# RWKV-5 attention and a wave MLP on one core: w loaded as one row and spread by a product, with a new order in the opening

## The chip, the cores and the metric

The kernel runs on one core of one Trainium2 chip. The metric is device time in microseconds of one execution, the median over the runs. TensorE is called PE here (PEld is its loading of weights), VectorE DVE, ScalarE ACT, GpSimd POOL, and SyncE SP; SP computes nothing and issues transfers. ACT and POOL issue transfers too, each on its own queue.

## The reference

r, k and v are [4, 8, 768, 48] f32 (batch, heads, tokens, columns of a head), w and u are [8, 48]. The first stage runs a decaying state over the tokens, the second mixes tokens and channels:

```python
for t in range(S):
    cur = np.einsum('bhd,bhe->bhde', u[None] * kt, vt)
    y[:, :, t] = np.einsum('bhd,bhde->bhe', rt, state + cur)
    state = w[None, :, :, None] * state + np.einsum('bhd,bhe->bhde', kt, vt)
...
theta = x @ w_theta                      # x: y as [4, 768, 384]
zr, zi = x * np.cos(theta), x * np.sin(theta)
y = einsum('ts,bsd->btd', w_tok_r, zr) + einsum('ts,bsd->btd', w_tok_i, zi)
u = x + y
return u + np.maximum(u @ w_ch, 0.0)     # f32 [4, 768, 384]
```

## The kernel before

The recurrence is done in blocks. The 768 tokens of a batch element are three pairs of chunks of 128 tokens, and a load brings 256 tokens of all eight heads (384 KB). Within a block the decay is taken off beforehand: k is multiplied by powers of w that fall with the token's place (table `kpow`, or `kpow_c` for pairs laid out in the other way) and r by the inverse ones (`rpow`). The products are `Kw` and `Rw` (L546). PE turns them (`flip`, L484), ACT or DVE copies the turned blocks to `KT` and `RT` (L499, L500), PE forms scores `RT` by `KT` (L592), and DVE masks these into `mAT` (L601). The bonus term with u takes an elementwise product `PD` of `RT` and `KT` (L608, for the first pair on POOL), which PE sums against the columns of u over w, `uw` (L625, the diagonal product). State, outputs, x, theta, sine and cosine, z, the token mixing (L859) and the channel product (L891) follow, batch element after batch element.

The powers are exponentials: `tok_f` holds factors of the token's place, `lw_f` the logarithm of w, and six activations (L388) write exp(factor * log w) into the tables. For that w is loaded onto all 128 partitions, as 128 equal rows (L300, `w_row`, which lies in a buffer of `z`). A second, small load (L395) brings w and u as `wu`, four rows of two heads each; PE turns it (L402, the flip of wu), and from that come `wup`, `uw` (L407, L422) and, on ACT, `lwu` (L410) and `w256`.

Some products do no work: `unread` (L291) multiplies a tile of zeros, six and eight times in the opening (tasks 3 and 4, the warm-ups), and after the tasks named in `IDLE`, as often as its third number says.

The order is written out by hand. Every step is a task with a number, by its place in the source; `ORDER` lists the numbers in the order in which the instructions are issued, each to the queue of its engine; `WAYS` picks one of a task's alternatives by a digit (for L395: 0 is SP, 1 is ACT). `BANKS` gives PSUM banks to PE's tasks in the order in which they ask, and `AFTER` adds waits, such as that of the first cast of weights (task 48, on POOL) for the first loads of r and k (tasks 34 and 35). Each engine works through its queue in order and waits at an instruction until what it needs is there.

Of the kernel before, what the change touches and what calls it, by code (L numbers as in the profile page):

```python
# [14 lines left out]
F32 = mybir.dt.float32  # L15
# [3 lines left out]
Act = mybir.ActivationFunctionType  # L19

PE, DVE, ACT, POOL, SP, NONE = "PE", "DVE", "ACT", "POOL", "SP", "NONE"
# [7 lines left out]


ORDER = [
# [42 lines left out]
]  # L74

WAYS = (
    "000000000000000000000000001100000000000000100101001000010000001001000000000200000010"
    "000000011000000000000000000001000100000000000000100100000100100000000000000000000000"
    "000000000000100000000000000000110000000000002100100000000000000000001000000000000000"
    "000000010000000000000000000100000000000010000000000100000000000000000000011011000000"  # L80
# [17 lines left out]
]  # L98

IDLE = [  # L100
    (3, 0, 1), (4, 1, 3), (71, 2, 2), (116, 6, 3), (76, 1, 3), (49, 4, 2), (51, 1, 1),
    (94, 5, 4), (97, 4, 1), (157, 3, 1),
]

# [59 lines left out]
def rows_of(w, n):  # L164
    return dataclasses.replace(w, ap=[[0, n]] + [list(x) for x in w.ap])
# [13 lines left out]
def kernel(  # L179
# [13 lines left out]
    nc = tc.nc  # L193
    B, H, S, D = r.shape
    HD = H * D
    C = 128
# [7 lines left out]
    sb = ctx.enter_context(tc.tile_pool(name="sb", bufs=1))  # L204
    ps = ctx.enter_context(tc.tile_pool(name="ps", bufs=1, space=bass.MemoryType.PSUM))
    P = Plan()
# [13 lines left out]
    place = sb.tile([C, 2, C], BF16, name="place")  # L220
    mask01 = sb.tile([C, 2, C], BF16, name="mask01")
    zero = sb.tile([C, C], BF16, name="zero")
    col_i = sb.tile([C, C], mybir.dt.int32, name="col_i")
    thr = sb.tile([C, 3], F32, name="thr")
    pi2 = sb.tile([C, 1], F32, name="pi2")
# [46 lines left out]
    def act(n, fn, more=51):  # L272
        return (ACT, n / 1.2 + more, False, fn)
# [21 lines left out]

    def setup():
        if WARM:
            P.add((DVE, 120, False, lambda: nc.vector.memset(zero, 0.0)), wr=["zero"],
                  prio=-3e4, name="zero")
        P.add((ACT, 2950, False, lambda: nc.scalar.dma_start(out=w_row, in_=rows_of(w, C))),  # L300
              wr=["w_row"], prio=-3e4, name="w_row", kind="small")
        P.add((DVE, 60, False, lambda: nc.vector.memset(pi2, math.pi / 2.0)), wr=["pi2"],
              prio=-210, name="pi2")
# [69 lines left out]
        def pads(ts):  # L373
# [4 lines left out]
        P.add(pool(260 * NR, lambda: pads(Rws)), wr=[("Rw", i) for i in range(NR)], prio=-202,  # L378
              name="pads")

        P.add(act(HD, lambda: nc.scalar.activation(
            lw_f, w_row, Act.Ln), 93), rd=["w_row", "set"], wr=["lw_f"], prio=-200,
            name="ln")
        for i, (dst, nm, j, col) in enumerate((
                (kpow, "kpow", 0, 2), (kpow, "kpow", 1, 3), (rpow, "rpow", 0, 0),
                (rpow, "rpow", 1, 1), (kpow_c, "kpow_c", 0, 5), (kpow_c, "kpow_c", 1, 6))):
            to = dst[:, j] if nm[-1] == "c" else dst[:, :, j, :]
            P.add((ACT, 510, False, lambda to=to, col=col: nc.scalar.activation(  # L388
                to, lw_f, Act.Exp, scale=tok_f[:, col:col + 1])),
                rd=["lw_f", "tok_f"], wr=[(nm, j), ("exp", i)],  # L390
                prio=-199 + 0.1 * i, name="pow")

        for i, src in enumerate((w, u)):
            def wu_load(eng, i=i, src=src):
                return eng.dma_start(out=wu[i * HP:(i + 1) * HP, :, :D],  # L395
                                     in_=src.rearrange("(a b) d -> a b d", b=2))
            P.add([(SP, 450, False, lambda f=wu_load: f(nc.sync)),
                   (ACT, 2700, False, lambda f=wu_load: f(nc.scalar))], rd=["wu0"],
                  wr=[("wu", i)], prio=-90 + 0.0035, desc=(0, 1, 20), name="wu", kind="small")

        def wu_flip():
# [557 lines left out]
```

## Time and profile before

| What | us |
|---|---|
| median of two runs | 141.53 |
| lowest and highest | 141.36, 141.69 |
| span of the profiled execution, from its first to its last instruction | 139.4 |
| busy in that span: PE, DVE, ACT | 126.8, 112.0, 78.4 |
| busy in that span: POOL | 60.4 |
| start of the first scores on PE (L592) | 13.69 |
| last instruction of the first setup on DVE before it waits for PE | 4.54 |

The profile gives the span of the execution it shows and no other time for it; the runs' median lies 2.1 us above that span. PE is busy for 91% of the span, and the granted clock in its rows is 1.00 throughout. How to read the lines below: an instruction row gives its start, its length, engine, line, operation, output<-input and count, and in brackets how long the engine had stood idle and for whom. `x3` counts instructions. In a row of issues the last number is the time from issue to landing.

### The profile page before, as it was taken

The page shows a single profiled execution, that of the slowest core. Times are in us where ns is not written, and L with a number is a line of the kernel's source. Part 1 is how long each engine was busy: PE and PEld are TensorE (multiplying, and loading weights), DVE is VectorE, ACT ScalarE, POOL GpSimd, SP SyncE. Part 2 cuts the span into 40 slices and gives each one's busy share as a digit, 9 for nine tenths or more (in the row PEclk, how much of TensorE's full clock was granted, in tenths as well). Part 3 has the DMA queues.
Part 4 walks back from the last instruction along what each step waited for, and adds up shares of the span by engine and source line. Part 5 has one row for each costly group of instructions (what it writes and reads, how often), then busy time and mean ns, then how long its engine had stood idle before and what let it go on. Part 6 is the DMA issues. An engine that isn't in the chain of part 4 may idle for free.

```text
span 139.4 us, 4508 instructions
## 1 busy us (share of the span) xinstructions
PE 126.8 (91%) x1896; PEld 83.5 (60%) x1896; DVE 112.0 (80%) x207; ACT 78.4 (56%) x147; POOL 60.4 (43%) x63
## 2 busy tenths in 40 slices
PE   1775999899798999999999999999999999999980
PEld 0134657677464777676766667776566675666630
DVE  5329998797989999899966979999989997256470
ACT  2466369987760657898895779556501351810110
POOL 5025776735423069999300059997302722000000
PEclk9999999999999999999999999999999999999999
DMA  3999999999999995039799998969993718605344
GB/s 35 247 253 251 267 250 263 219 236 228 234 268 244 271 135 78 5 121 261 195 168 229 207 203 147 158 142 119 314 208 104 152 34 211 172 0 169 61 164 175
DMA packets 64941, 25.08 MB, mean 180 GB/s; under 512 B 59416, under 2 KB 64920, under 8 KB 64920
## 3 DMA queue, kind: packets, MB, share of 16 engines
q1 hardware_dynamic: 62320, 21.63, 73.2%
q0 software_dynamic: 2432, 2.95, 12.7%
q10 hardware_dynamic: 168, 0.20, 1.4%
q8 instruction: 15, 0.25, 0.8%
q14 instruction: 6, 0.05, 0.1%
HBM read 20.25 MB, written 4.72 MB: 179 GB/s over the span
## 4 chain that ended last, share of the span: by engine, by line
PE 77%; DVE 8%; DMA 4%; ACT 3%; POOL 2%; issue 2%; ACTq 0%; POOLq 0%; DVEq 0%
PE bank L859 31%; PE bank L484 10%; PE bank L891 8%; PE bank L822 8%; PE bank L592 4%; DMA wu<-in_w_dram 4%; PE bank L658 3%; PE bank L747 3%; DVE Rw L546 2%; PE bank L625 2%; PE bank L799 2%; PE bank L763 2%; PE bank L734 2%; POOL PD L608 2%; DVE z L837 1%
## 5 line engine op out<-in xcount | busy, mean ns | idle before, releaser
L859 PE MATMUL bank<-z,WrT 128*128 128x384 bf16 x144 | 46.8, 326 | 0.7 <-DVE z L837 0.7
L859 PE MATMUL bank<-z,WiT 128*128 128x384 bf16 x144 | 46.8, 326 | 0.0
L634 POOL TENSOR_TENSOR yd<-dg,vb 128x768 bf16<-128x768 f32 x11 | 16.2, 1471 | 7.3 <-ACT vb L568 3.2
L859 PEld LDWEIGHTS <-WiT 128*128 128x128 bf16 x144 | 14.1, 98 | 8.4 <-issue 0.8
L859 PEld LDWEIGHTS <-WrT 128*128 128x128 bf16 x144 | 14.0, 98 | 8.3 <-ACT WrT L499 0.3
L601 DVE TENSOR_TENSOR mAT<-bank,mask 128x512 bf16<-128x512 f32 x28 | 18.1, 680 | 0.1
L608 POOL TENSOR_TENSOR PD<-RT,KT 128x1024 bf16<-128x1024 bf16 x5 | 10.6, 2124 | 15.4 <-ACT dg L630 14.3
L877 DVE TENSOR_TENSOR uu_all<-bank,x 128x384 bf16<-128x384 f32 x24 | 13.1, 552 | 4.8 <-PE bank L859 4.4
L837 DVE TENSOR_TENSOR z<-x,trig 128x1536 bf16<-128x1536 bf16 x12 | 13.0, 1081 | 4.9 <-ACT trig L829 2.6
L499 ACT ACTIVATE KT<-bank 128x1024 bf16<-128x1024 bf16 x11 | 11.2, 1022 | 8.1 <-PE bank L484 7.8
L829 ACT ACTIVATE trig<-bank,pi 128x384 f16<-128x384 f32 x24 | 13.6, 583 | 2.7 <-PE bank L822 2.5
L833 ACT ACTIVATE trig<-bank 128x384 f16<-128x384 f32 x24 | 11.3, 490 | 6.3 <-PE bank L822 6.3
L822 PE MATMUL bank<-Wth,xT 128*128 128x384 bf16 x72 | 14.3, 326 | 0.0
L891 PE MATMUL bank<-Wch,uu_all 128*128 128x384 bf16 x72 | 13.8, 326 | 0.1
L601 DVE TENSOR_TENSOR mAT<-bank,mask_c 128x512 bf16<-128x512 f32 x20 | 13.0, 681 | 1.1 <-PE bank L592 0.9
L291 PE MATMUL bank<-zero 128*128 128x512 bf16 x35 | 10.7, 430 | 3.0 <-DVE thr L338 3.0
L499 ACT ACTIVATE RT<-bank 128x1024 bf16<-128x1024 bf16 x10 | 10.2, 1021 | 5.2 <-PE bank L484 5.2
L900 DVE SCALAR_TENSOR_TENSOR fin_all<-bank,uu_all 128x384 f32<-128x384 f32 x22 | 11.4, 550 | 0.9 <-PE bank L891 0.8
L546 POOL TENSOR_TENSOR Kw<-ld,kpow 128x768 bf16<-128x768 f32 x3 | 7.8, 2588 | 6.2 <-DMA ld<-in_k_dram 4.7
L592 PE MATMUL bank<-RT,KT 64*64 64x128 bf16 (+1 forms) x304 | 8.8, 220 | 1.3 <-ACT RT L499 1.1
L891 PEld LDWEIGHTS <-uu_all 128*128 128x128 bf16 x72 | 6.6, 97 | 4.2 <-ACT uu_all L499 0.5
L822 PEld LDWEIGHTS <-xT 128*128 128x128 bf16 x72 | 6.5, 98 | 4.0 <-DMA xT<-x 0.4
(111 smaller groups left out, 216.1 us busy)
## 6 DMA issues: line engine op xcount, KB each, us to landing
ld<-in_r_dram SPq DMA_DIRECT2D x12, 384.0 KB, 6.5
out_dram<-fin_all SPq DMA_DIRECT2D x11, 384.0 KB, 3.0
ld<-in_k_dram SPq DMA_DIRECT2D x7, 384.0 KB, 7.5
ld<-in_v_dram SPq DMA_DIRECT2D x7, 384.0 KB, 5.9
ld<-in_k_dram SPq DMA_DIRECT2D x10, 192.0 KB, 4.8
ld<-in_v_dram SPq DMA_DIRECT2D x10, 192.0 KB, 4.7
uu_all<-in_moe_w_tok_r_dram POOLq DMA_DIRECT2D x1, 384.0 KB, 7.2
z<-in_moe_w_tok_i_dram POOLq DMA_DIRECT2D x1, 384.0 KB, 6.5
```

The lines of the kernel that those rows point to most:

```text
L484: ins = [nc.tensor.matmul(bank16(tok)[:, i * C:(i + 1) * C], s, ident, is_transpose=True, start=(i == 0), stop=(i == n - 1)) for i, s in e ...
L499: ways = [act(n * C, lambda: nc.scalar.activation(dst, src(), Act.Copy)), dve(n * C, lambda: nc.vector.tensor_copy(dst, src()), 1.0 if pai ...
L592: ins.append(nc.tensor.matmul(to[:, hp * C:(hp + 1) * C], a, m, start=(hp == 0), stop=(hp == HP - 1), skip_group_check=True))
L601: mask01[:, j] if pairs else mask_c): nc.vector.tensor_mul(
L608: return eng.tensor_mul(flat[2], flat[0], flat[1])
L634: return eng.tensor_mul(yd.rearrange("p a b d -> p (a b) d"), wide(dg, D), vb.rearrange("p a b d -> p (a b) d"))
L822: ins = [nc.tensor.matmul(bank(th)[:, :HD], xT[:, t, dk, :], Wth[:, dk, :], start=(dk == 0), stop=(dk == ND - 1)) for dk in range(ND)]
L829: P.add(act(HD, lambda th=th, t=t, trig=trig: nc.scalar.activation(trig[:, t, 0], bank(th)[:, :HD], Act.Sin, bias=pi2), 144), use=[th], rd ...
L837: P.add(dve(4 * HD, lambda trig=trig, pr=pr: nc.vector.tensor_mul(z[:, 2 * pr:2 * pr + 2], bc(x[:, 2 * pr:2 * pr + 2], 2, 2), trig), 2.0, ...
L859: ins.append(nc.tensor.matmul(bank(tm)[:, :HD], (WrT, WiT)[ri][:, so, to * C:(to + 1) * C], z[:, so, ri], start=(part == 0 and i == 0), st ...
L877: P.add(dve(HD, lambda tm=tm, t=t, to=to, un=un: nc.vector.tensor_add(un[:, t], bank(tm)[:, :HD], x[:, to])), use=[tm], rd=[("x", xi, pr, ...
L891: ins = [nc.tensor.matmul(bank(tf)[:, :HD], uT[:, t, dk, :], Wch[:, dk, :], start=(dk == 0), stop=(dk == ND - 1)) for dk in range(ND)]
```

## The change

The log of w is now computed from one row on one partition, and a product with a row of ones spreads it over all 128 partitions into a PSUM bank (bank 7). The six table activations read that bank. The two small loads of `wu` go from ACT's queue to POOL's.

```diff
 ORDER = [
-    1, 18, 35, 14, 27, 7, 34, 6, 17, 8, 110, 5, 9, 0, 10, 3, 26, 13, 15, 16, 109, 19, 28, 20,
+    1, 18, 34, 14, 7, 35, 6, 17, 8, 36, 5, 9, 0, 10, 3, 27, 26, 13, 15, 11, 16, 109, 19, 4, 20,
...
 WAYS = (
-    "000000000000000000000000001100000000000000100101001000010000001001000000000200000010"
+    "000000000000000000000000002200000000000000100101001000010000001001000000000200000010"
...
 IDLE = [
-    (3, 0, 1), (4, 1, 3), (71, 2, 2), (116, 6, 3), (76, 1, 3), (49, 4, 2), (51, 1, 1),
+    (3, 0, 1), (71, 2, 2), (116, 6, 3), (76, 1, 3), (49, 4, 2), (51, 1, 1),
...
+    ones = sb.tile([1, C], F32, name="ones")
...
-            P.add((DVE, 120, False, lambda: nc.vector.memset(zero, 0.0)), wr=["zero"],
+            P.add((DVE, 120, False, lambda: (nc.vector.memset(ones, 1.0),
+                                             nc.vector.memset(zero, 0.0))), wr=["zero"],
                   prio=-3e4, name="zero")
-        P.add((ACT, 2950, False, lambda: nc.scalar.dma_start(out=w_row, in_=rows_of(w, C))),
+        P.add((ACT, 2950, False, lambda: nc.scalar.dma_start(out=w_row[:1], in_=rows_of(w, 1))),
...
-        P.add(act(HD, lambda: nc.scalar.activation(
-            lw_f, w_row, Act.Ln), 93), rd=["w_row", "set"], wr=["lw_f"], prio=-200,
-            name="ln")
+        lw = bank_t[7][:, :HD]
+
+        def spread():
+            a = nc.scalar.activation(lw_f[:1], w_row[:1], Act.Ln)
+            nc.tensor.matmul(lw, ones, lw_f[:1].rearrange("p h d -> p (h d)"), start=True,
+                             stop=True)
+            return a, a
+        P.add(act(HD, spread, 93), rd=["w_row", "set", "zero"], wr=["lw_f"], prio=-200,
+              name="ln")
...
-                to, lw_f, Act.Exp, scale=tok_f[:, col:col + 1])),
+                to, lw.rearrange("p (h d) -> p h d", h=H), Act.Exp,
+                scale=tok_f[:, col:col + 1])),
...
             P.add([(SP, 450, False, lambda f=wu_load: f(nc.sync)),
-                   (ACT, 2700, False, lambda f=wu_load: f(nc.scalar))], rd=["wu0"],
+                   (ACT, 2700, False, lambda f=wu_load: f(nc.scalar)),
+                   (POOL, 900, False, lambda f=wu_load: f(nc.gpsimd))], rd=["wu0"],
```

In the rows below the lines of the changed kernel are its own; the numbers behind names tell buffers apart, and those of rings stand one higher in the changed kernel.

ACT's queue from the start to the copies of the first turned blocks, before and then changed (`z` is the buffer of `w_row` and `lw_f`, `bank_68` is bank 7):

```order
L300 DMA z_156<-in_w_dram 128x384
L395 DMA wu<-in_u_dram 4x2x48
L310 ACT_TABLE_LOAD
L395 DMA wu<-in_w_dram 4x2x48
L381 ACTIVATE z_156<-z_156 128x384
L388 ACTIVATE kpow<-z_156,tok_f 128x8x48
L388 ACTIVATE kpow_c<-z_156,tok_f 128x384
L410 ACTIVATE lwu<-bank_61 128x4
L388 ACTIVATE rpow<-z_156,tok_f 128x8x48
```

```order
L302 DMA z_157<-in_w_dram 1x384
L312 ACT_TABLE_LOAD
L386 ACTIVATE z_157<-z_157 1x384
L396 ACTIVATE kpow<-bank_68,tok_f 128x8x48 x2
L396 ACTIVATE rpow<-bank_68,tok_f 128x8x48 x2
L420 ACTIVATE lwu<-bank_62 128x4
L509 ACTIVATE KT_121<-bank_62 128x1024
L509 ACTIVATE RT_117<-bank_63 128x1024
L396 ACTIVATE kpow_c<-bank_68,tok_f 128x384 x2
```

The loads of `wu` are gone from ACT, both parts of `kpow` and of `rpow` come first, `lwu` comes behind them, and `kpow_c` behind the copy to `RT`. `KT`'s bank, 62, is now the one that `lwu` reads.

DVE's queue from `uw`'s memset to the first masked scores, before and then changed:

```order
L362 MEMSET uw 128x4
L366 MEMSET Sd_142 128x192
L366 MEMSET Sd_143 128x192
L366 MEMSET Sd_144 128x192
L366 MEMSET Sd_145 128x192
L407 COPY wup<-bank_61 128x4
L422 TENSOR_TENSOR uw<-bank_61,wup 64x4 x2
L546 TENSOR_TENSOR Kw_106<-ld_88,kpow 128x8x2x48
L546 TENSOR_TENSOR Rw_104<-ld_89,rpow 128x8x2x48
L346 TENSOR_SCALAR mask_72<-col_i,thr 128x128 x2
L546 TENSOR_TENSOR Kw_107<-ld_91,kpow 128x8x2x48
```

```order
L364 MEMSET uw 128x4
L348 TENSOR_SCALAR mask_72<-col_i,thr 128x128 x2
L368 MEMSET Sd_143 128x192
L368 MEMSET Sd_144 128x192
L368 MEMSET Sd_145 128x192
L368 MEMSET Sd_146 128x192
L417 COPY wup<-bank_62 128x4
L432 TENSOR_TENSOR uw<-bank_62,wup 64x4 x2
L556 TENSOR_TENSOR Kw_107<-ld_89,kpow 128x8x2x48
L556 TENSOR_TENSOR Rw_105<-ld_90,rpow 128x8x2x48
L556 TENSOR_TENSOR Kw_108<-ld_92,kpow 128x8x2x48
```

The masks move ahead of the memsets, and Kw of pair 1 follows Rw of pair 0 directly.

POOL's queue, from the last pad to the first products, before and then changed:

```order
L374 MEMSET Kw_108 128x16x16
L374 MEMSET Kw_109 128x16x16
L453 DMA uu_all<-in_moe_w_tok_r_dram 128x2x768
L546 TENSOR_TENSOR Rw_105<-ld_92,rpow 128x8x2x48
L608 TENSOR_TENSOR PD_123<-RT_116,KT_120 128x1024
```

```order
L376 MEMSET Kw_109 128x16x16
L376 MEMSET Kw_110 128x16x16
L404 DMA wu<-in_u_dram 4x2x48
L404 DMA wu<-in_w_dram 4x2x48
L463 DMA uu_all<-in_moe_w_tok_r_dram 128x2x768
L556 TENSOR_TENSOR Rw_106<-ld_93,rpow 128x8x2x48
L618 TENSOR_TENSOR PD_124<-RT_117,KT_121 128x1024
```

The two loads of `wu` stand ahead of the first cast of weights. On POOL, Rw of pair 1 waits by semaphore for Rw of pair 0 on DVE, and PD for Kw of pair 1, in both kernels.

On PE, before: seven products with zeros, the flip of `wu`, eleven more with zeros, then K's flip. Changed: seven with zeros, the product that spreads log w, eight with zeros, the flip of `wu`, then K's flip, which takes the bank of the flip of `wu` and so waits for `lwu`. SP's queue begins with the loads r, k, r, k, v, k, v before and with k, r, v, k, r, v, k in the changed kernel; from the eighth load on both are the same, as is everything on the other engines behind the places shown.

2 rows, old and new, of the table ORDER are left out of this document.

## The prediction

> **What bounds the kernel now.** I read the page's head first, then busy time by stretches of ten microseconds, then the chain of work that ended last, then the five engines' timelines of the opening, and the DMA view last.
>
> ```profile
> span 139.4 us, 4508 instructions
> ```
>
> ```profile
> 0.00:10.00 10.00, 5.29 (x18) 1.95 (x19) 3.44 (x27) 4.18 (x8) 2.82 (x13) 1.00 0.83 176
> 10.00:20.00 10.00, 8.25 (x159) 5.37 (x158) 9.97 (x14) 5.45 (x12) 6.24 (x6) 1.00 1.16 257
> ...
> 30.00:40.00 10.00, 9.14 (x120) 6.23 (x120) 9.19 (x11) 7.29 (x15) 4.70 (x4) 1.00 1.13 234
> ...
> 50.00:60.00 10.00, 10.00 (x202) 7.07 (x199) 9.56 (x17) 7.41 (x14) 9.75 (x9) 1.00 0.38 45
> ```
>
> After the stretch's length come the busy times of PE, PEld, DVE, ACT and POOL, then clock, DMA share and GB/s. From 50 us on PE has no gap, so whatever the opening gains or loses by then goes through to the end. The change touches only the opening, up to the first scores. The chain there:
>
> ```profile
> 2.50 5.25 DMA wu<-in_w_dram
> ...
> 7.88 0.21 PE bank L402
> ...
> 9.42 0.51 ACT kpow L388
> ...
> 10.83 0.95 DVE Rw L546
> 11.78 1.98 DVE mask L346 x2
> 13.76 0.88 DVE Kw L546
> ...
> 14.77 2.13 POOL PD L608
> ...
> 16.95 0.35 PE bank L625 x8
> ```
>
> It begins with the load of w's columns, lands at 7.75, and by the flip (L402) and the tables reaches Kw of pair 0. Then Rw, the masks, Kw of pair 1, PD on POOL and the diagonal product (L625) follow. I compare that product's start, 16.95, before and after, since PE stands almost without a gap behind it.
>
> **The change part by part.** Edits with one answer first. The `ones` memset delays `zero` and so the warm-up products.
>
> ```profile
> 3.70 0.84 DVE L366 MEMSET Sd<- 128x192 uint32 x4
> ```
>
> A memset of 192 columns takes 0.21, so 128 columns cost at most that; I take 0.1. Two of w's tables (kpow_c) move behind RT's copy on ACT, where ACT idles before KT of pair 1; they cost nothing, and about 1.0 if that gap closed. v of pair 0 goes ahead of k and r of pair 1, so r becomes the fifth load.
>
> ```profile
> 15.80 1.02 ACT L499 ACTIVATE KT<-bank 128x1024 bf16<-128x1024 bf16 x1 [2.15 <-PE bank L484]
> ```
>
> ```profile
> 7.08 1.37 SPq L433 DMA_DIRECT2D ld<-in_v_dram  x1
> ```
>
> ```profile
> ld<-in_v_dram SPq DMA_DIRECT2D x1, 384.0 KB, 5.8
> ```
>
> The fifth load now is that v: 7.08 + 5.8 = 12.9. Less the 0.75 by which the stream comes forward (below) r lands at 12.15, just before POOL can take it at 12.3: free, with little to spare.
>
> *w as one row.* The 128-row load is what moved first:
>
> ```profile
> q10 hardware_dynamic: 93, 0.12, 50.2%
> q1 hardware_dynamic: 638, 0.24, 46.9%
> ```
>
> This is the DMA from 3 to 5 us: ACT's queue (q10) still holds half of it, SP's loads (q1) share the rest. One row lands earlier, but w's landing isn't on the path any more, because the product that spreads it stands on PE behind seven warm-up products:
>
> ```profile
> 2.97 3.17 PE L291 MATMUL bank<-zero 128*128 128x512 bf16 x7 [2.97 <-DVE thr L338]
> ...
> 8.01 2.55 PE L291 MATMUL bank<-zero 128*128 128x512 bf16 x11
> ```
>
> They end at 6.14 + 0.1 = 6.25, less a short drain: the spread starts at 6.15. No f32 product of 384 columns is in this trace. The lower end is a bf16 one, 0.33 (row L859); the upper end is three early warm-up products, 3 x 3.17/7 = 1.36. I take 0.75, nearer the lower, since the warm-ups quicken from 0.45 to 0.23 each by 8.01: 6.9.
>
> ```profile
> L859 PE MATMUL bank<-z,WrT 128*128 128x384 bf16 x144 | 46.8, 326 | 0.7 <-DVE z L837 0.7
> ```
>
> The Trainium skill, "FP8 and Floating Point Precision", TensorE Precision Notes, says a true FP32 product makes four passes through the array. By it an estimate would be 4 x 0.33 = 1.3, against 0.75, and everything below stood 0.55 later; no row here shows it.
>
> *Eight warm-ups, then the flip.* Eight at 2.55/11 = 0.23 take 1.85 (3.6 if the clock stayed low): PE is free for the flip at 8.75. The four exps that Kw and Rw need start at 6.9 and take 0.5 each on ACT (the chain's 0.51), ending at 8.95, early enough. From the flip's start to uw's end the rows say:
>
> ```profile
> 8.31 0.34 DVE L422 TENSOR_TENSOR uw<-bank,wup 64x4 bf16<-64x4 f32 x2
> 9.96 0.96 DVE L546 TENSOR_TENSOR Kw<-ld,kpow 128x768 bf16<-128x768 f32 x1 [1.30 <-ACT kpow L388]
> ```
>
> 8.65 - 7.88 = 0.77, so uw ends at 9.52 and Kw, which stands behind it on DVE, starts at 9.55 instead of 9.96. lwu waits for uw on ACT, and K's flip now waits for lwu, since both use one PSUM bank: 9.75, well before Kw's end. So the tables' gain of about one us is cut to 0.4 by the flip, which comes behind eight warm-ups.
>
> *wu by GpSimd.* POOL issues both when its last pads are written.
>
> ```profile
> 1.59 1.05 POOL L374 MEMSET Kw<- 128x256 bf16 x4
> ...
> 9.26 0.89 POOL L453 DMA_DIRECT2D uu_all<-in_moe_w_tok_r_dram  x1 [6.61 <-DMA ld<-in_k_dram]
> ```
>
> ```profile
> Wth<-in_moe_w_theta_dram POOLq DMA_DIRECT2D x1, 288.0 KB, 7.6
> Wch<-in_moe_w_ch_dram POOLq DMA_DIRECT2D x1, 288.0 KB, 4.2
> ```
>
> Second issue at 2.64 + 0.85 = 3.5. Landing is 4.2 after issue at the least for a cast, 7.6 in a loaded queue. A transfer of 1.5 KB should be nearer 4.2: 7.7, one us before PE is free. That cover is thin; the ends are 7.7 and 11.1, and below 7.7 nothing is gained. The first cast behind them on POOL waits for loads anyway.
>
> *Masks early.* Two mask operations of 0.28 go where DVE stood idle from the last memset's end, 4.54, to the flip, 7.88: free. In their old place they cost 1.98, and the reason matters:
>
> ```profile
> L346 DVE TENSOR_SCALAR mask<-col_i,thr x2: 281/1074/1868, 11.7 to 11.9; 128x128 bf16<-128x128 int32 x2
> ```
>
> ```profile
> 11.88 1.80 POOL L546 TENSOR_TENSOR Rw<-ld,rpow 128x768 bf16<-128x768 f32 x1 [1.72 <-DVE Rw L546]
> ```
>
> The second mask took 1.87 because POOL was writing Rw of pair 1 from 11.88 to 13.68. That block changes sides. Kw of pair 1 now follows Rw of pair 0 on DVE at once, while POOL's Rw still waits for that Rw's semaphore. What happens then stands later in the trace:
>
> ```profile
> 50.97 1.80 DVE L546 TENSOR_TENSOR Rw<-ld,rpow 128x768 bf16<-128x768 f32 x2
> 52.70 0.68 DVE L608 TENSOR_TENSOR PD<-RT,KT 128x1024 bf16<-128x1024 bf16 x1
> ```
>
> ```profile
> 51.06 4.00 POOL L546 TENSOR_TENSOR Kw<-ld,kpow 128x768 bf16<-128x768 f32 x1
> ```
>
> DVE began first, and POOL's operation took 4.00 instead of 1.80: it stood until DVE's three were through. So Rw of pair 0 ends at 9.55 + 1.82 (9.96 to 11.78 now) = 11.37, Kw of pair 1 at 12.27, POOL's Rw runs 12.3 to 14.1, and PE's flip of it starts at 14.15. Now it starts at 14.04:
>
> ```profile
> 14.04 0.62 PE L484 MATMUL bank<-ident,Rw 128*128 128x128 bf16 x8
> ...
> 16.04 0.82 PE L291 MATMUL bank<-zero 128*128 128x512 bf16 x3
> ```
>
> Between that flip and the diagonal product PE has 2.82 us of its own work (14.04 to 16.86), fillers included, so the product starts at 16.97 against 16.95. The opening gains nothing: 0.4 won on the tables, lost on the port.
>
> *Loads earlier.* 191 of 192 KB of w are no longer moved. At 257 GB/s, the stretch from 10 to 20, that brings the stream of loads forward by 0.75; q10's hold on the engines before 5 us may add as much. It can pay where a load is waited for:
>
> ```profile
> 20.93 3.07 SPq L433 DMA_DIRECT2D ld<-in_k_dram  x1
> ```
>
> ```profile
> ld<-in_k_dram SPq DMA_DIRECT2D x1, 384.0 KB, 13.4
> ```
>
> ```profile
> 34.47 1.80 POOL L546 TENSOR_TENSOR Kw<-ld,kpow 128x768 bf16<-128x768 f32 x1 [1.42 <-PE bank L484]
> ```
>
> ```profile
> 35.01 2.08 DVE L546 TENSOR_TENSOR Rw<-ld,rpow 128x768 bf16<-128x768 f32 x1
> ```
>
> ```profile
> 37.14 0.62 PE L484 MATMUL bank<-ident,Rw 128*128 128x128 bf16 x8 [0.60 <-DVE Rw L546]
> ```
>
> The k load issued at 20.93 lands at 34.33, POOL starts on it at 34.47, and DVE's Rw behind it takes 2.08 instead of 0.95; PE waits 0.60. With the load 0.75 earlier DVE's Rw ends up to 0.75 sooner. I take 0.5, between nothing (POOL meets another DVE operation) and PE's 0.60. What is late next there is z on DVE.
>
> **Sum.** Opening 0.0, loads -0.5: span 138.9. The median of the two runs, 141.53, lies 2.1 above the span of the profile; the page gives no other time for that execution, so I carry the 2.1: **141.0**.
>
> **Rivals.**
> *The columns land late (slower).* Place: POOL's two issues. The Trainium skill, "SBUF — State Buffer", section "SBUF: two separate sides", says that a DMA issued by GpSimd cannot write its descriptors while VectorE holds the shared port pair in a two-port mode, and tells of 620 ns growing to 3100. For it here: POOL and DVE do block each other in the rows above, and DVE runs without a pause until 4.54, in the change 0.6 longer for masks and ones. Against: no issue in the rows above is longer than 0.89. As a mechanism here: both issues start at 5.15, the second at 6.0, landing 4.2 later at 10.2; the flip at 10.3, uw's end 11.05, Kw 11.1 instead of 9.96. POOL's Rw then ends at 15.65, the product comes at 18.5, 1.55 late; less 0.5: **142.5**. It decides from a landing later than about 9.2, which puts Kw back at 10.1. The same follows from a slow spread and a clock that stays low, 8.75 becoming 10.5.
> *POOL takes the port first.* If Rw on POOL starts at 11.4, before Kw of pair 1, it ends at 13.2; the flip comes 2.26 behind Rw of pair 0 as now (11.78 to 14.04), at 13.63, the product at 16.45: 0.5 gained. With the loads' full 0.75 and part of PE's later waits, **140.1**. The start order of the rows speaks against it.
> *The change doesn't do what it says.* The earlier loads meet DVE elsewhere, and the opening is even: **141.5**.
>
> **How the numbers follow.** Forecast 0.5 (own range 140.4 to 141.5), late columns 0.15, POOL first 0.15, nothing 0.2. The range 139.7 to 142.4 holds all of the forecast and of nothing, most of POOL first and not quite half of the late columns. A difference under 2%, 2.8 us, is about what a measurement of this kernel cannot tell from no change. Below 138.7 lies only a tail of POOL first, 0.03; above 144.4 a tail of late columns (11.1 and the low clock together), 0.02; within 2%, 0.95.
>
> **What would show it.** In the changed profile: the spread on PE at 6.1 to 6.2 and its length; the flip at 8.7 to 9.0, started by PE and not by a DMA; Kw on DVE at 9.5; two masks of 0.28; POOL's Rw of pair 1 ending behind Kw of pair 1, about 14.1, with 2.7 on its row instead of 1.80; the diagonal product near 17.0; POOL's Kw at 33.7 instead of 34.47. I'm wrong if the flip waits for wu (first rival), if POOL's Rw ends before 13.5 (second), or if PE's gaps after 20 us change by more than the 0.5 given to the loads.

## The result, and the profile after

The changed kernel takes 148.04 us (147.15 and 148.93), the kernel before 141.53: a ratio of 1.044 (1.036 to 1.053). Six more runs later gave a median of 148.41 (147.02 to 153.41). The forecast was 141.0. A ratio compares undisturbed runs of the two kernels; medians and ranges below are of all runs, and of its 62 later runs the kernel before, too, had four at 147.8 to 148.5, of which no trace was kept.

Busy time by stretches, changed kernel (length; busy time of PE, PEld, DVE, ACT, POOL; clock, DMA share, GB/s):

```profile
0.00:10.00 10.00, 6.90 (x15) 2.24 (x16) 3.43 (x26) 3.80 (x6) 4.15 (x15) 1.00 0.97 208
10.00:20.00 10.00, 6.88 (x93) 4.17 (x91) 6.71 (x11) 4.17 (x7) 5.99 (x4) 1.00 1.23 258
...
30.00:40.00 10.00, 5.89 (x121) 4.45 (x122) 8.81 (x10) 5.52 (x12) 6.66 (x7) 1.00 1.08 233
40.00:50.00 10.00, 8.70 (x70) 6.25 (x69) 7.15 (x9) 5.45 (x10) 0.43 (x1) 0.83 0.92 201
50.00:60.00 10.00, 10.00 (x173) 7.28 (x172) 9.39 (x18) 4.18 (x6) 2.27 (x3) 1.00 0.15 24
```

There are two losses. From 10 to 20 PE does 6.88 where it did 8.25, and from 30 to 40 5.89 where it did 9.14, with a clock of 0.83 behind that. From 50 on PE is full, as before. The chain shows both places:

```profile
7.84 3.49 PE bank L292 x8
12.09 0.96 DVE Kw L556
13.05 0.88 DVE Rw L556
14.01 2.45 POOL Rw L556
...
29.69 1.19 issue
...
35.67 5.59 DVE z L847
```

The warm-ups stand on the path where a load stood, and z takes 5.59 us. The opening on PE:

```profile
3.10 3.17 PE L292 MATMUL bank<-zero 128*128 128x512 bf16 x7 [3.10 <-DVE thr L340]
6.20 1.65 PE L387 MATMUL bank<-z,ones 1*128 1x384 f32 x2
7.78 3.56 PE L292 MATMUL bank<-zero 128*128 128x512 bf16 x8
11.26 0.22 PE L412 MATMUL bank<-ident_f,wu 8*128 8x8 f32 x1
...
19.16 0.34 PE L635 MATMUL bank<-uw,PD 128*128 128x2 bf16 x8
```

The eight warm-ups take 0.44 each, as at half clock, and not 0.23; the flip of wu starts at 11.26 and the diagonal product at 19.16, 2.2 later than before. The clock column says 1.00 all the same; here the length of equal products tells the clock, the column does not.

The second place: z on DVE before, z on DVE after, then POOL and PE after.

```profile
31.80 0.95 DVE L837 TENSOR_TENSOR z<-x,trig 128x1536 bf16<-128x1536 bf16 x1
```

```profile
35.59 5.66 DVE L847 TENSOR_TENSOR z<-x,trig 128x1536 bf16<-128x1536 bf16 x1
```

```profile
33.95 1.48 POOL L644 TENSOR_TENSOR yd<-dg,vb 128x768 bf16<-128x768 f32 x1 [3.25 <-ACT dg L640]
35.36 0.77 POOL L463 DMA_DIRECT2D z<-in_moe_w_tok_r_dram  x1
36.12 0.72 POOL L463 DMA_DIRECT2D x<-in_moe_w_tok_i_dram  x1
36.86 3.56 POOL L556 TENSOR_TENSOR Kw<-ld,kpow 128x768 bf16<-128x768 f32 x2
```

```profile
41.30 0.32 PE L869 MATMUL bank<-z,WrT 128*128 128x384 bf16 x1 [4.51 <-DVE z L847]
```

POOL's two Kw run without a gap; before they stood 1.42 and 4.72 us apart from what preceded them, waiting for loads (the row of the first names a bank of PE, but its load landed at 34.33, just before its start at 34.47). z ends at 41.25, which is 0.83 after the second Kw ends (36.86 + 3.56 = 40.42). PE stands 4.51 for it.

Why the loads are there is seen at SP's start, the third and fourth load before and after:

```profile
1.88 3.91 SPq L433 DMA_DIRECT2D ld<-in_r_dram  x1
5.83 1.21 SPq L433 DMA_DIRECT2D ld<-in_k_dram  x1
```

```profile
1.87 1.01 SPq L443 DMA_DIRECT2D ld<-in_v_dram  x1
2.92 1.29 SPq L443 DMA_DIRECT2D ld<-in_k_dram  x1
```

With w's 128 rows in the transfers the third load's issue took 3.91 and held everything behind it; with one row it takes 1.01, and the fourth to the thirteenth load go out 2.4 to 3.0 earlier. The k load of POOL's first Kw, further on:

```profile
18.00 1.44 SPq L443 DMA_DIRECT2D ld<-in_k_dram  x1
```

```profile
ld<-in_k_dram SPq DMA_DIRECT2D x1, 384.0 KB, 7.2
```

It lands at 25.2; before it landed at 34.33.

From span to span, 139.4 to 147.2: the diagonal product starts 2.2 later, from there to the first product of the token mixing it takes 22.1 instead of 16.0, and from there to the end 105.9 instead of 106.5.

### The profile page after: what moved, and what is told of

It is laid out like the page before. It is cut to its first block, busy times and chain, and to the rows that moved or that the text cites. A ratio compares the mean times of both kernels' runs of the same rounds, so it can differ in the third digit from the quotient of the medians.

```text
span 147.2 us, 4507 instructions
## 1 busy us (share of the span) xinstructions
PE 130.4 (89%) x1895; PEld 85.7 (58%) x1895; DVE 113.0 (77%) x208; ACT 78.5 (53%) x147; POOL 62.0 (42%) x65
## 3 DMA queue, kind: packets, MB, share of 16 engines
HBM read 20.06 MB, written 4.72 MB: 168 GB/s over the span
## 4 chain that ended last, share of the span: by engine, by line
PE 83%; DVE 9%; POOL 2%; issue 2%; ACT 1%; DVEq 0%; POOLq 0%
PE bank L869 33%; PE bank L494 11%; PE bank L901 8%; PE bank L292 7%; PE bank L832 7%; PE bank L602 5%; DVE z L847 4%; PE bank L668 3%; PE bank L757 2%; PE bank L635 2%; POOL Rw L556 2%; PE bank L809 2%; PE bank L773 1%; DVE mAT L611 1%; PE bank L744 1%
## 5 line engine op out<-in xcount | busy, mean ns | idle before, releaser
L869 PE MATMUL bank<-z,WrT 128*128 128x384 bf16 x144 | 47.3, 329 | 4.5 <-DVE z L847 4.5
L869 PE MATMUL bank<-z,WiT 128*128 128x384 bf16 x144 | 47.3, 329 | 0.0
L847 DVE TENSOR_TENSOR z<-x,trig 128x1536 bf16<-128x1536 bf16 x12 | 16.5, 1377 | 4.9 <-ACT trig L843 2.4
L292 PE MATMUL bank<-zero 128*128 128x512 bf16 x32 | 11.7, 496 | 3.1 <-DVE thr L340 3.1
L556 POOL TENSOR_TENSOR Rw<-ld,rpow 128x768 bf16<-128x768 f32 x4 | 7.9, 1974 | 6.8 <-DVE Rw L556 6.8
L602 PEld LDWEIGHTS <-KT 64*64 64x64 bf16 (+1 forms) x304 | 6.1, 103 | 5.4 <-issue 4.8
L691 POOL CAST Sd<-F 64x192 bf16<-64x192 f32 x3 | 1.0, 342 | 19.1 <-ACT F L710 17.1
```

What stands on the lines that cost most here:

```text
L292: ins = [nc.tensor.matmul(bank_t[k][:, :wide * C].rearrange("p (a c) -> p a c", a=wide), zero, bc(zero, 1, wide), start=True, stop=True, s ...
L602: ins.append(nc.tensor.matmul(to[:, hp * C:(hp + 1) * C], a, m, start=(hp == 0), stop=(hp == HP - 1), skip_group_check=True))
L847: P.add(dve(4 * HD, lambda trig=trig, pr=pr: nc.vector.tensor_mul(z[:, 2 * pr:2 * pr + 2], bc(x[:, 2 * pr:2 * pr + 2], 2, 2), trig), 2.0, ...
L869: ins.append(nc.tensor.matmul(bank(tm)[:, :HD], (WrT, WiT)[ri][:, so, to * C:(to + 1) * C], z[:, so, ri], start=(part == 0 and i == 0), st ...
```

## The experiments

The theories: **A**, the opening is late because the flip of wu, and on DVE Kw behind it, stand behind warm-ups that run at half clock. **B**, z loses the port to POOL's two Kw, which are ready too early (port is here, as in the prediction, the name for what makes operations of DVE and POOL wait for each other in its rows); **B2**, they are ready early because the 128-row load is gone. **C**, rival of B: z is late only because the opening is. **D**, the clock comes up by windows of 3.41 us that run free of the kernel. In `ORDER` 3 and 4 are the warm-ups, 19 ln and the spread, 28, 29, 33 and 30 the flip of wu, wup, uw and lwu, 24 and 25 kpow_c, 69 to 74 Kw and Rw of pair 0 and their flips; 108 and 151 are the first two z, 236 and 368 POOL's two Kw.

**The flip of wu first** (`BANKS` exchanges the second and third bank with it).

```diff
-    1, 18, 34, 14, 7, 35, 6, 17, 8, 36, 5, 9, 0, 10, 3, 27, 26, 13, 15, 11, 16, 109, 19, 4, 20,
-    21, 110, 22, 23, 28, 29, 33, 30, 48, 69, 111, 70, 71, 152, 113, 72, 73, 74, 24, 112, 25,
+    1, 18, 34, 14, 7, 35, 6, 17, 8, 36, 5, 9, 0, 10, 3, 27, 26, 13, 15, 11, 16, 109, 19, 28, 4, 20,
+    21, 110, 22, 23, 29, 33, 30, 48, 69, 111, 70, 71, 152, 113, 72, 73, 74, 24, 112, 25,
```

> The changed kernel with the flip of wu issued ahead of the eight warm-ups instead of behind them. Theory A (PE's in-order queue: the flip stands behind eight warm-ups of 0.44 us): the flip starts at 7.8 to 8.0, where the spread product ends, uw ends at 8.6, and Kw of pair 0 is bound by its tables (kpow ends 8.9), so it starts near 9.0 instead of 12.09. The eight warm-ups then run from about 8.1 to 11.6, so PE's flip of Kw starts at 11.6 instead of 13.20: 1.6 us off the opening. Rival (wu's columns come late, not the order): the flip still starts near 11. For the second loss, theory B (POOL's two Kw, ready behind its casts, take the shared port ahead of z on DVE, whatever the opening does): z of the first batch element's first pair is blocked again for more than 3 us and the time is 145 to 147. Rival C (the stall of z comes from the late opening alone): z takes 0.95 and the time is 141 to 142.

Median 145.26 (140.28 to 146.40, 4 runs). In the profile the flip starts at 8.09, Kw at 8.96, and the diagonal product at 17.24, 1.9 earlier: A holds. z took 0.96, which is not what B expected here, yet this run took 144.62, which is not what C expected: this profile fits neither. PE stood 1.11 us within its scores at 27.3, and the clock was at half from 28.6 to 32.0.

**z before POOL's first Kw.**

```diff
-    (34, 48), (35, 48), (70, 113), (112, 82), (155, 85), (168, 134), (406, 559), (448, 565),
+    (34, 48), (35, 48), (108, 236), (70, 113), (112, 82), (155, 85), (168, 134), (406, 559), (448, 565),
```

> The changed kernel with one wait more: the first Kw on POOL after its casts (the one at 36.86) waits for z of the first pair on DVE (the one at 35.59 that took 5.66 us). Theory B (the shared port: z stood behind two Kw of POOL that were ready at once): z takes 0.95 or less from the end of its trig table, PE's idle stretch of 4.51 us shrinks below 0.7, the granted clock stays at 1.00 between 40 and 46, and the time is 142.5 to 144.0, 4 to 5.5 us under the changed kernel. Rival (z waited for something else, the port is only where it shows): z stays at 4 us or more, the time at 147 to 149. The opening is untouched: Kw of pair 0 at 12.1 in either.

Median 144.23 (141.32 to 144.91, 4 runs), 4 under the changed kernel. z took 0.95 and POOL's Kw still follow the casts at once:

```profile
35.39 0.95 DVE L847 TENSOR_TENSOR z<-x,trig 128x1536 bf16<-128x1536 bf16 x1
```

The diagonal product stays at 19.24. B holds: the wait that was added costs POOL nothing and takes the second loss away. POOL's two casts still stand ahead of Kw, the first 0.23 before z, so it was Kw, and not the issuing of the casts, that kept z.

**w over 128 rows again, no spread.**

```diff
-        P.add((ACT, 2950, False, lambda: nc.scalar.dma_start(out=w_row[:1], in_=rows_of(w, 1))),
+        P.add((ACT, 2950, False, lambda: nc.scalar.dma_start(out=w_row, in_=rows_of(w, C))),
...
-        lw = bank_t[7][:, :HD]
...
+            lw_f, w_row, Act.Ln), 93), rd=["w_row", "set"], wr=["lw_f"], prio=-200,
...
-                to, lw.rearrange("p (h d) -> p h d", h=H), Act.Exp,
+                to, lw_f, Act.Exp,
```

> The changed kernel without the spread product: w is loaded onto 128 partitions again and ln runs over 128 rows; the order, the loads, the warm-ups and POOL's queue stay as changed. ln then starts when the load lands, near 5.7, and the eight warm-ups follow the seven at about 6.2 without a break. Theory A1 (the spread product keeps the clock low, being one row of 128 in f32): the eight warm-ups come up to speed within 1 to 2 us, the flip of wu starts between 8.0 and 9.0 and Kw of pair 0 by 9.8. Theory A2 (the clock comes up at a time of its own, whatever PE does): the eight still run at 0.44 us each, the flip starts at 9.7 and Kw at 10.5. The second loss by theory B stays in both (146 to 147); by rival C (it comes from the late opening) it goes, 141 to 143.

Median 142.36 (141.30 to 148.65, 10 runs), 1.003 of before (1.000 to 1.006). So all of the loss hangs on w as one row. Fifteen warm-ups took 4.78 us; the flip waits for wu until 9.04. POOL waits for its loads again (the first row names PE; its load landed at 35.0):

```profile
35.16 1.80 POOL L550 TENSOR_TENSOR Kw<-ld,kpow 128x768 bf16<-128x768 f32 x1 [1.91 <-PE bank L488]
41.70 1.96 POOL L550 TENSOR_TENSOR Kw<-ld,kpow 128x768 bf16<-128x768 f32 x1 [4.73 <-DMA ld<-in_k_dram]
```

I had expected theory B's loss to stay here, and by that expectation this run speaks for C: the order of the loads, which this kernel keeps, isn't what makes Kw ready. B2 and C are told apart further down.

**The order of the loads alone**, in the kernel before.

```diff
-    1, 18, 35, 14, 27, 7, 34, 6, 17, 8, 110, 5, 9, 0, 10, 3, 26, 13, 15, 16, 109, 19, 28, 20,
-    4, 24, 36, 29, 33, 30, 23, 21, 22, 48, 69, 152, 25, 70, 71, 111, 11, 113, 72, 73, 74, 112,
+    1, 18, 34, 14, 27, 7, 35, 6, 17, 8, 36, 5, 9, 0, 10, 3, 26, 13, 15, 16, 109, 19, 28, 20, 4,
+    24, 110, 29, 33, 30, 23, 21, 22, 48, 69, 111, 25, 70, 71, 152, 11, 113, 72, 73, 74, 112,
```

> The kernel before with one part of the change: SP issues its first nine loads in the changed order (k, r, v of pair after pair). Nothing else is touched. Theory B in its strict form (earlier k loads alone make POOL's two Kw ready at once, and z is blocked): z of the first pair on DVE takes more than 3 us and the time is 144 to 146. Rival (the order of the loads changes little, since the Kw of before wait for loads that are issued much later): 141 to 142, with z at 0.95.

Median 141.97 (141.25 to 149.48, 10 runs), 1.002 of before (0.999 to 1.005). The order is harmless. But in this profile, with no spread, the eleven later warm-ups took 4.46 us instead of 2.55: a late clock is not the spread's alone.

**The changed kernel again.**

> The changed kernel once more, unchanged, in more runs, since its time so far rests on two. Theory D (the time depends on when the clock comes up, and that on a window of 3.41 us that runs free of the kernel: the trace's clock record has the clock of the changed kernel up at 11.17, down at 41.89, nine windows later, and up again at 45.30): the runs spread over groups, near 141 where the clock is up before the eight warm-ups, near 144 where it is not, and 147 to 149 where PE also stands still long enough to lose the clock; the median falls to 143 to 145. Rival (148 is the kernel's own time, given by its order): all runs between 147 and 149.

Median 148.41 (147.02 to 153.41, 6 runs), 1.041 of before (1.036 to 1.046). The rival is nearer, and D in this form is wrong: no run was near 141 or 144, but three of the six took more than the rival's 149. z took 5.53 in this profile too.

**The spread first**, 19 moved ahead of 3.

```diff
-    1, 18, 34, 14, 7, 35, 6, 17, 8, 36, 5, 9, 0, 10, 3, 27, 26, 13, 15, 11, 16, 109, 19, 4, 20,
+    1, 18, 34, 14, 7, 35, 6, 17, 8, 36, 5, 9, 0, 10, 19, 3, 27, 26, 13, 15, 11, 16, 109, 4, 20,
```

> The changed kernel with the spread product moved ahead of the seven warm-ups, so that all fifteen warm-ups run without a break behind it, from about 4.8. Theory D with the rider that the spread product does not count as work for the clock: a stretch of 6.5 us of warm-ups fills some window wherever that begins, so the clock is up before the last warm-up in every run, at 10.7 at the latest; the flip of wu starts at 9.6 to 11.0 (11.26 as changed), the tables are done at 7.0, Kw of pair 0 at 10.0 to 11.8; time 141 to 143.5. Rival (the clock comes up at 11 whatever PE does before): the flip at 11.3, Kw at 12.1, the time as the changed kernel's.

Median 147.36 (146.62 to 148.15, 4 runs), 1.042 of before (1.035 to 1.049). The opening did what was expected, the time did not:

```profile
4.72 5.00 PE L292 MATMUL bank<-zero 128*128 128x512 bf16 x15
9.66 0.22 PE L412 MATMUL bank<-ident_f,wu 8*128 8x8 f32 x1
```

The clock is up at 7.98 and the diagonal product at 17.55, 1.6 earlier; but z takes 5.66 again. The order of the loads alone had z pass behind a later opening (18.04), so C falls.

**Tables first**, the columns behind the flips (`BANKS` gives the flip of wu bank 0 there).

```diff
-    1, 18, 34, 14, 7, 35, 6, 17, 8, 36, 5, 9, 0, 10, 3, 27, 26, 13, 15, 11, 16, 109, 19, 4, 20,
-    21, 110, 22, 23, 28, 29, 33, 30, 48, 69, 111, 70, 71, 152, 113, 72, 73, 74, 24, 112, 25,
+    1, 18, 34, 14, 7, 35, 6, 17, 8, 36, 5, 9, 0, 10, 19, 3, 27, 26, 13, 15, 11, 16, 109, 4, 20,
+    21, 110, 22, 23, 24, 25, 48, 69, 111, 70, 71, 152, 113, 72, 73, 74, 28, 29, 33, 30, 112,
```

> As the kernel with the spread first, and besides the flip of wu, wup, uw and lwu stand behind the flips of Kw and Rw of pair 0 instead of ahead of them (uw is first needed by the diagonal product), and kpow_c comes right behind the other tables. Theory A (PE's and DVE's order: Kw stood behind columns that it doesn't need): Kw of pair 0 starts when its loads have landed and the tables are there, near 7, five us before the changed kernel; the flip of Kw is bound by the end of the warm-ups (8.5 to 11.4) and the diagonal product comes at 14 to 16.5 (19.16 as changed, 16.95 before); time 139 to 142. Rival (the opening is bound by the loads): Kw at 9 or later, the diagonal product not before 17, time 142 or more.

Median 145.65 (140.08 to 146.05, 4 runs). Kw starts at 5.91 and the diagonal product at 16.44, as A has it; the time expected, 139 to 142, was missed, since z took 5.67 in the profile. One run of the four was over 5 us faster than the others.

**The spread over 128 rows**, 127 of them zeros; twice, for two phases of the window.

```diff
-    ones = sb.tile([1, C], F32, name="ones")
+    ones = sb.tile([C, C], F32, name="ones")
...
-            nc.tensor.matmul(lw, ones, lw_f[:1].rearrange("p h d -> p (h d)"), start=True,
+            nc.tensor.matmul(lw, ones, lw_f.rearrange("p h d -> p (h d)"), start=True,
```

> The changed kernel with the spread product over 128 rows instead of one: 127 rows of lw_f are zeros and the ones stand on all 128 partitions, so it computes the same table at the same size. Theory D1 (a product over one row does not count as work for the clock, a product over 128 rows does): PE is then at work without a break from 3.2, and the clock record has the clock up at the first or second window's end after that, between 5.8 and 9.2. Theory D2 (an f32 product does not count, however many rows; or the clock is late for another reason): the clock comes up at 10.5 to 13.9 unless the phase is lucky, that is unless a window's end falls between 5.5 and 7.0.

> The spread product over 128 rows once more, for another phase of the clock's window (in the first run a window ended at 6.69, which lies in the lucky stretch of 5.5 to 7.0). D1 (128 rows count as work): clock up between 5.8 and 9.2. D2 (they do not): up at 10.5 to 13.9 unless a window's end falls between 5.5 and 7.0. Which one the window's phase allows is read from the later clock steps, which lie whole windows of 3.41 us apart.

145.38 and 147.26, one run each. The first clock came up at 6.69, in the stretch that says nothing, the second at 8.69, as D1 has it; what that means stands below. z took 5.66 and 5.67.

**The 128-row load put back beside the one row.**

```diff
+    rows = sb.tile([C, HD], F32, name="rows")
...
-        P.add((ACT, 2950, False, lambda: nc.scalar.dma_start(out=w_row[:1], in_=rows_of(w, 1))),
+        P.add((ACT, 2950, False, lambda: (
+            nc.scalar.dma_start(out=w_row[:1], in_=rows_of(w, 1)),
+            nc.scalar.dma_start(out=rows.rearrange("p (h d) -> p h d", h=H),
+                                in_=rows_of(w, C)))[:1] * 2),
```

> The changed kernel with the old load of w over 128 partitions issued besides the one-row load, into a tile that nothing reads. Theory B2 (the second loss comes from the 192 KB that the change took out of the transfers: SP's third load took 3.91 us to issue behind them, and 1.01 without them, so that all later loads come 2.9 us earlier and POOL's two Kw are ready as soon as its casts are out, ahead of z): SP's third load takes 3.7 to 3.9 again, the fourth is issued near 5.6 instead of 2.92, POOL waits for its Kw's loads again (1 to 2 us, then 4 to 5), z takes 0.95 and PE does not stand for it; the opening stays as late as in the changed kernel (diagonal product 18 to 19.5); time 142 to 144.5. Rival (it is the lateness of the opening, or the spread product itself, that brings z behind Kw): z at 5.6 again, time 147 or more.

```profile
1.87 1.90 SPq L447 DMA_DIRECT2D ld<-in_v_dram  x1
3.81 2.58 SPq L447 DMA_DIRECT2D ld<-in_k_dram  x1
```

Half of what was expected: the fourth load goes out at 3.81, between 2.92 and 5.83. The runs split: 141.78 to 142.54 in four, 145.99 to 149.08 in four (median 144.26). The profile is of the first kind, with z at 0.95. The clock was early (6.86), so the opening was not late, which I had not expected. What z did in the other runs isn't seen. B2 holds for this profile; the kernel with 128 rows again, which leaves the spread out too, bears it out more plainly.

**Tables first, and z before POOL's first Kw**: the two diffs above together.

> The kernel with the tables first (spread ahead of the warm-ups, columns behind the flips of Kw and Rw) and with the wait of POOL's first Kw for z of the first pair. Theories A and B together (the opening gains where Kw does not stand behind columns, and is only paid back where z stands behind POOL): Kw of pair 0 near 7, diagonal product at 14 to 16.5, z at 0.95, no half clock at 38 to 41; span 137.5 to 139.5, time 139.4 to 141.4, at or under the kernel before. Rival (what the opening gains is waited for elsewhere, at the loads of the second batch element or the casts): 142 or more with z at 0.95.

Median 139.75 (139.47 to 141.37, 12 runs), 0.991 of before (0.987 to 0.995): below both kernels, though by less than 2% against the one before. z took 0.95, the clock up from 8.05 to the end, the diagonal product at 15.70:

```profile
5.91 0.96 DVE L556 TENSOR_TENSOR Kw<-ld,kpow 128x768 bf16<-128x768 f32 x1 [0.85 <-ACT kpow L396]
```

```profile
32.28 1.81 POOL L556 TENSOR_TENSOR Kw<-ld,kpow 128x768 bf16<-128x768 f32 x1 [0.22 <-DMA ld<-in_k_dram]
```

In this profile the added wait was idle: z had ended at 31.75, and POOL's Kw waited for its load. That the wait matters is seen in the times alone: all twelve runs stayed under 141.4, where three of the four without it took over 145.

**The flip first, and z before Kw.**

> The changed kernel with its two repairs and nothing else: the flip of wu ahead of the eight warm-ups, and the wait of POOL's first Kw for z. Theories A and B: 1.6 us from the first and 4 to 5.5 from the second, 148.0 less 5.6 to 7.1, so 141 to 142.5 whatever the clock's phase; z at 0.95 in every profile. Rival (the single stop of PE at its scores near 28 us, which took the clock away in one run of the kernel with the flip first, keeps it up): 144 to 145.

Median 144.45 (141.35 to 144.56, 4 runs): the rival. z took 0.96, but the clock came up only at 14.15 and fell to half from 31.2 to 34.6, behind PE's stop of 1.2 us in its scores.

**Products of zeros while PE stands for z.**

```diff
-    (94, 5, 4), (97, 4, 1), (157, 3, 1),
+    (94, 5, 4), (97, 4, 1), (157, 3, 1), (178, 2, 19),
```

> The changed kernel with nineteen products of zeros (0.216 us each, 4.1 us) on PE right before the first token mixing, that is in the stretch in which PE stands for z. They take no wait away. Theory B with its second part (after 4.5 us without work the clock is at half for one window of 3.41 us, which costs half of it): z stays at 5.6, the clock in the stretches from 40 to 46 stays at 1.00, and the time falls by 1.5 to 2.0, to 145.3 to 146.5 where the clock's other dips stay away. Rival (the half clock costs nothing, since PE waits for other engines behind it anyway): 147 to 149 as the changed kernel.

Median 149.31 (145.49 to 151.46, 4 runs): by its time inconclusive, since in this profile the clock came up only at 22.50 and the diagonal product started at 22.55. Behind that the products did what they were put in for: z took 5.69, the clock was 1.00 from 40 to 48, and from the first mixing product to the end it took 104.9 us against 105.9. By these two profiles the half clock behind z costs about 1.0, not 1.7.

**Both z before POOL's Kw**, in the kernel with the tables first and z before POOL's first Kw.

```diff
-    (34, 48), (35, 48), (108, 236), (70, 113), (112, 82), (155, 85), (168, 134), (406, 559), (448, 565),
+    (34, 48), (35, 48), (108, 236), (151, 368), (70, 113), (112, 82), (155, 85), (168, 134), (406, 559), (448, 565),
```

> The faster kernel (tables first, first Kw of POOL behind z) with the same wait for the second pair: POOL's second Kw waits for the second z, which took 2.57 instead of 0.95 there and made PE stand for 0.72. If who asks for the port first decides, this z takes 0.95 too, PE's 0.72 shrinks below 0.2, and the time falls by 0.3 to 0.7 to 139.0 to 139.5. Rival (POOL's second Kw, now later, is waited for in its turn by PE's flip of it): PE's wait moves there and the time stays at 139.6 to 140.2.

Median 138.39 (138.06 to 141.07, 6 runs), 0.977 of before (0.972 to 0.983), a larger gain than expected. The second z takes 0.95, and POOL's second Kw waits for it:

```profile
37.08 1.81 POOL L556 TENSOR_TENSOR Kw<-ld,kpow 128x768 bf16<-128x768 f32 x1 [2.69 <-DVE z L847]
```

PE's wait of 0.72 is gone, and from the first mixing product on the kernel takes 104.4 instead of 105.8.

**What the profiles say together.** The row's start of z, and when the load of POOL's first Kw landed (issue plus time to landing), in the kernels without an added wait:

| profile | load landed | first cast of POOL | z starts | z takes | clock up | diagonal product | span |
|---|---|---|---|---|---|---|---|
| before | 34.3 | 31.56 | 31.80 | 0.95 | 6.67 | 16.95 | 139.4 |
| 128 rows again | 35.0 | 31.77 | 32.01 | 0.95 | 5.89 | 17.34 | 140.0 |
| order of loads alone | 34.2 | 33.00 | 33.24 | 0.95 | 12.01 | 18.04 | 140.4 |
| row load put back | 34.8 | 33.58 | 33.80 | 0.95 | 6.86 | 17.07 | 140.8 |
| flip first | 30.6 | 34.31 | 34.31 | 0.96 | 11.52 | 17.24 | 142.7 |
| changed | 25.2 | 35.36 | 35.59 | 5.66 | 11.17 | 19.16 | 147.2 |
| changed again | 25.2 | 35.81 | 36.17 | 5.53 | 11.97 | 19.25 | 147.7 |
| spread first | 30.8 | 33.33 | 33.56 | 5.66 | 7.98 | 17.55 | 144.8 |
| tables first | 30.8 | 32.53 | 32.76 | 5.67 | 10.49 | 16.44 | 144.1 |
| 128-row product | 30.1 | 32.02 | 32.24 | 5.66 | 6.69 | 16.68 | 143.6 |
| the same again | 31.0 | 33.91 | 34.14 | 5.67 | 8.69 | 17.67 | 145.5 |
| products of zeros | 24.1 | 38.34 | 38.57 | 5.69 | 22.50 | 22.55 | 149.2 |

One rule covers all twelve: where z starts 0.2 us or more behind POOL's first cast and Kw's load has landed by then, z stands until POOL's two Kw are through; where the load lands later, z passes. With the flip first the load was there too, but z started with the cast and passed. I read this as a port that goes to whoever is ready first and that POOL keeps over both Kw, although its row shows the first only 1.5 us later. The rows show who waits and how long; who holds the port in between they do not show.

## Why the prediction was wrong, point by point

- *The `ones` memset, 0.1*: 0.13. Right.
- *The spread starts at 6.15 and takes 0.75*: it starts at 6.20 and takes 1.65 at half clock (1.22 where the clock came up during it, at 6.86). Mis-sized by 0.9. The estimate by the Trainium skill, "FP8 and Floating Point Precision", TensorE Precision Notes, 1.3, was nearer than the value between my rows.
- *"Eight at 2.55/11 = 0.23 take 1.85 (3.6 if the clock stayed low)"*: 3.56. This is the first step that failed. I took the warm clock from a row that follows other products at other times. Flip at 11.26 for 8.75, Kw at 12.09 for 9.55, the diagonal product 2.2 late for 0.0. With z out of the way, that alone gave a median of 144.23.
- *wu by GpSimd, landing at 7.7, hidden*: the flip was started by PE, as said; with the flip first it waited for wu until 8.09. The first rival's mechanism is refuted: POOL's issues took 0.75 and 0.60 and did not wait for DVE. Its second cause, named in its last sentence (slow spread, low clock), is what happened in the opening; its 10.5 for the flip is 6.9 + 3.6 and so holds the low clock alone, and it came at 11.26.
- *Masks free, Kw of pair 1 takes the port before POOL's Rw, 2.7 on its row*: masks 0.28 each, 2.44 on the row. Right; the second rival is refuted.
- *"With the load 0.75 earlier DVE's Rw ends up to 0.75 sooner. I take 0.5"*: the step that decided. It counted w's bytes (191 KB at 257 GB/s), but the third load's issue had taken 3.91 us behind them, so the next ten loads went out 2.4 to 3.0 earlier, and the k load of POOL's Kw landed 9.1 earlier. And an earlier Kw on POOL was counted as a gain only. "What is late next there is z on DVE" named the victim without a price: PE stood 4.5 for it, and the half clock behind that cost about 1.0. The row of SP's third load was in the trace of before. The gain itself was there: PE's later waits for DVE, 0.60, 0.25 and 0.65 before, are gone in the changed kernel.
- *The chances*: the 0.02 for a slower kernel left out that a wait for a load had been keeping two engines apart.

What divides the 7.8 us of span: 2.2 to the diagonal product, 6.1 from there to the first mixing (4.5 by z, 1.0 by PE's longer stop within its scores, the rest spread), less 0.6 behind it, where the half clock's 1.0 is more than made up by PE's later waits of 1.5 that are gone.

## What to carry to other kernels

Before taking a load away, look at what was held up behind its issue, and then at what the earlier landings make ready: an engine that no longer waits may take a port from one on the critical path. A wait that costs the waiting engine nothing (POOL's Kw behind z) can be worth more than the change. Products that are to bring the clock up need an unbroken stretch long enough for any phase of its window (fifteen in a row had it up by 10.49 in the four kernels with the spread first), and nothing that the end waits for should stand behind them on PE.

## What the runs showed of the hardware

*The clock's window.* The trace's clock record has steps whole multiples of 3.41 us apart (changed kernel: up 11.17, down 41.89, up 45.30), at another phase in each run. Share of such a window in which PE was at products, leaving the spread out and counting it:

```
window that ended at        without spread  with it   clock after it
before            6.67           0.84         0.84    up
128 rows again    5.89           0.82         0.82    up
order of loads    5.18           0.65         0.65    stays low
fillers          12.27           0.79         0.79    stays low
flip, z before   10.73           0.81         0.96    stays low
changed           7.75           0.57         1.00    stays low
changed again     8.56           0.56         1.00    stays low
tables first      7.08           0.69         1.00    stays low
z before Kw       8.59           0.56         1.00    stays low
128-row product   8.69           0.69         1.00    up
```

In these rows a window lifts the clock from about four fifths of work on (0.82 did, 0.81 did not), if a product over one row does not count as work; one over 128 rows does count (one run shows the latter). The Trainium skill, "TensorE: Matmul & The Clock Gate", Part 1, has the free-running window of about 3.4 us and says its phase differs from run to run; these runs agree. It puts the penalty under 1% of a typical span; here, in the changed order of the opening, the diagonal product came at 17.07 with the clock up at 6.86 (row load put back), at 19.16 with 11.17 and at 22.55 with 22.50, 1.5 to 4% of the span.

*PE's stop within its scores.* In all but one profile PE stands between two of the sixteen scores of one product, waiting for nothing that the profile shows (1.19 in the chain above). It goes on 1.30 to 1.56 us after a 16 KB packet of the instruction queue ends (before: packet to 25.73, next score 27.08; changed: 29.32 and 30.88). The packet comes among the loads; the stop took 0.36 from start to start before and 1.40 in the changed kernel. That the packet is what PE waits for was not tested.
